# The maxima of two heads in four neighbouring rows of a score stack, returned by one transfer

## The chip, the core and the metric

The kernel runs on one core of a Trainium2 chip. The metric is the device time of one execution in microseconds (us). A core has five engines with their own instruction queues: TensorE (PE; its weight loads are listed apart as PEld), VectorE (DVE), ScalarE (ACT), GpSimd (POOL) and SyncE (SP). SP and ACT also issue the transfers between DRAM and the on-chip memory (SBUF), which 16 DMA engines carry out. Matmul results lie in PSUM.

## The reference, cut to what matters

```python
# A: attention over a sliding block of W = 256 keys, H = 32 heads of Dh = 16, S = 2048, D = 512
qkv = (x @ wqkv).reshape(B, S, 3, H, Dh)
scores = einsum("bhqd,bhkd->bhqk", q, k) * Dh ** -0.5
mask = (i - j >= 0) & (i - j < W)
p = softmax(where(mask, scores, -1e9))
a = einsum("bhqk,bhkd->bhqd", p, v) @ wo
# B: layer norm, Dense(1792), gelu, Dense(512)
b = gelu(layernorm(x) @ w1 + b1) @ w2 + b2
g = sigmoid((x * gate_w).sum(-1))
return g * a + (1 - g) * b
```

All inputs are float32. The softmax takes off each query's maximum; the change touches how these maxima reach the matmul that subtracts them.

## The kernel before

**Stages.** First come the projections (`qk_unit`, `v_unit`, L302 to L340), 12 matmuls of 128x512 each, and from 50 us on the first scores between them. From about 145 to 480 us run the attention of eight *head pairs* p (four heads each, two stacks of two heads) and, between its matmuls, the first layer of the MLP (`mlp1_unit`, L639). The rest is the second layer and the output projection. Numbers are held as a high and a low part of float32r, so each product is made of three matmuls.

**The stack.** `qk` (L166) is one SBUF tile of 128 partitions and four planes of 2048 columns: planes 0 and 1 hold q for the two stacks (`qs`), planes 2 and 3 hold k (`ks`). A head takes 48 partitions (three copies of 16 rows of high and low parts). In a plane the first head has partitions 14 to 61, the second 64 to 111. The two partitions behind a head's 48 belong to its maxima: in q the high and the low part of the maximum, in k the constant -1, so that the matmul of `st_pair` (L418: partitions 0 to 63 and 64 to 113) gives score minus maximum. `s_pair` (L362: 0 to 61 and 64 to 111) leaves those partitions out and gives plain scores, of which DVE takes the row maxima (L371, L372).

**Transfers.** The projections are written to the DRAM tiles `qkd[g, t]` (L162; t is 0 for q and 1 for k), eight heads of 50 rows each. `gaps` (L219) fills rows 48 and 49 of every head with -1, from partitions 112 to 127 of a k plane; it is issued once for each of four groups g. `load_stacks` (L344) brings the columns a to a + n of a head pair into the stack: 98 rows of DRAM (48, the two gap rows, 48) to partitions 14 to 111, both planes of t in one transfer, k first and then q. For the first pair there are four pairs of transfers of 512 columns, afterwards 56 pairs of 256 columns.

**The maxima.** Every four query blocks `put_max` (L376) runs a chain: `parts` splits 16 maxima of each of 128 partitions into high and low on POOL, `turn` transposes them on DVE, `put` writes them to a DRAM tile `md` (16 KB), and `rest` (L393 to L397) reads them back into the q planes, the high parts to partitions 62 and 112, the low ones to 63 and 113: two transfers of 8 KB, each with two outer rows. There are 32 such chains.

**Order.** In the attention stage the string `ORDER` sets the sequence of `s_pair` (S), `st_pair` (T), `pv` (P) and filler matmuls of the MLP (f). `CHAIN` gives the places after which the four steps of a chain are issued. `block` (L726) issues the stack loads of the next head pair at every second T block, and scores run ahead of T by `NB - LAG` = 10 blocks. All of SP's transfers go out in program order. A transfer reports on one of eight completion semaphores in turn (DMAHW0 to DMAHW7, shared by SP and ACT), and waits until the transfer eight places before it has landed.

Of the kernel before, what the change touches and what calls it, by code (L numbers as in the profile page):

```python
# [19 lines left out]
S = 2048  # L20
D = 512
H = 32
DH = 16
# [9 lines left out]
VW = 17  # L33
VR = 560
EPS = 1e-5
NEG = -3.0e38
# [25 lines left out]
def gated_mix_kernel(ctx, tc: tile.TileContext, xt, x2, wq0, wqk, wv, wo, xa, gw, w1, w2, b1, b2, out):  # L62
# [7 lines left out]
    def nm(s):  # L70
        uid[0] += 1
        return f"{s}_{uid[0]}"
# [56 lines left out]
    def f32(t):  # L129
        return t.bitcast(F32)  # L130
# [88 lines left out]
    def gaps(g):  # L219
        for t in range(2):  # L220
            sp.dma_start(f32(view(qkd[g, t], [50 * S, HG], [S, 2], [1, S], off=48 * S)), f32(ks[0][112:128]))

# [89 lines left out]
    def qk_out(g, t, c, o):  # L312
# [5 lines left out]
        def put(eng, k, s):  # L318
            eng.dma_start(f32(view(d, [S, DH], [50 * S, HG], [1, C], off=k * DH * S + c * C)), f32(s))

# [6 lines left out]
    def double(g, c, t):  # L327
        fr, to = (f32(view(qkd[g, t], [S, DH], [50 * S, HG], [1, C], off=k * DH * S + c * C)) for k in (0, 1 + t))
        sp.dma_start(to, fr)
# [14 lines left out]
    def load_stacks(p, a, n):  # L344
        g, j = divmod(p, 2)
        held_cols[p] = a + n
        for t in (1, 0):
            src = view(qkd[g, t], [S, 98], [100 * S, 2], [1, n], off=4 * j * 50 * S + a)
            sp.dma_start(f32(qk[14:112, 2 * t:2 * t + 2, a:a + n]), f32(src))

    mxs, done = {}, set()

    def s_pair(p, qb, pr):
# [6 lines left out]
        for e in range(2):  # L360
            r, k = ((0, 62), (64, 112))[e]
            pe.matmul(o[:, e, :n], qs[pr][r:k, qb * 128:qb * 128 + 128], ks[pr][r:k, t0:t0 + n],  # L362
                      start=True, stop=True)
# [12 lines left out]
    def put_max(p, a):  # L376
        mx = mxs[p][:, :, :, a:a + 4]
        sm = {}
        md = dram.tile([2, 2, 2, 4, 128], F32R, name=nm("md"))

        def parts():
            m = sm["m"] = small("nm", 2, (128, 2, 2, 2, 4), F32R)
            pool.tensor_copy(m[:, 0], mx)
            lo_part(m[:, 1], mx, m[:, 0], pool)

# [7 lines left out]
        def rest():  # L393
            done.add(("m", p, a // 4))
            for k in range(2):
                src = view(md, [512, 2], [1024, 2], [1, 512], off=2048 * k)
                sp.dma_start(f32(qk[62 + k:113 + k:50, :2, a * 128:a * 128 + 512]), f32(src))  # L397

# [573 lines left out]
```

## Time and profile before

| | before |
|---|---|
| median of 3 runs | 688.86 us (688.81 to 690.28) |
| the profiled execution | 689.64 us; its span 687.8 us, granted clock 0.999 |
| DMA | 137.91 MB in 89620 packets, mean 200 GB/s |
| DVE L372, row maxima | 144.1 us busy, 208 of 693 ns |
| POOL L422, masks | 74.2, 62.2 and 49.3 us busy in its three groups |
| ACT L420, exponentials | 76.5, 66.2 and 50.7 us busy in its three groups |

The span is the time from the first to the last instruction on the core; the execution's own time also holds what lies around it. Busy time is the time in which an engine works on instructions. It does not tell which engine sets the end: that is read from the chain of work that ended last, and from what an engine waited for. In a group's row stand the line, engine and operation, what is written and read, the count, the busy time and the mean of one instruction, and the idle time ahead with what ended it. SPq and ACTq rows are instructions that issue transfers.

### The profile page before, as it was taken

How to read it: one execution, taken by the hardware profiler on the slowest of the kernel's cores; microseconds unless marked ns; L12 is line 12 of the kernel's file. 1: busy time of each engine (PE TensorE's matmuls, PEld its weight loads, DVE VectorE, ACT ScalarE, POOL GpSimd, SP SyncE). 2: the span in 40 equal slices, each digit the busy share in tenths (PEclk: the TensorE clock that was granted, in tenths of full speed). 3: DMA queues.
4: the chain of work that ended last, by engine and by line, in shares of the span. 5: the costliest groups of instructions: out<-in, count | busy, mean ns of one | idle time of the engine just before them, and what ended most of it. 6: DMA issues, size and time to landing. Idle time of an engine off the chain costs nothing.

```text
span 687.8 us, 15593 instructions
## 1 busy us (share of the span) xinstructions
PE 681.1 (99%) x5674; PEld 535.5 (78%) x5674; DVE 476.4 (69%) x970; ACT 384.6 (56%) x637; POOL 265.9 (39%) x622
## 2 busy tenths in 40 slices
PE   9999999999999999999999999999999999999997
PEld 6887777877768777877787777777787888888886
DVE  6737789968777787777686877855575545556454
ACT  6438453457677776877758777687633224123231
POOL 6800156426666664765656566568000000000000
PEclk9999999999999999999999999999999999999999
DMA  8998888786575767566676555527876450841801
GB/s 322 354 290 266 278 262 267 217 253 224 176 211 173 247 211 228 174 214 188 190 240 207 168 185 153 178 96 240 288 238 204 143 173 5 275 126 41 253 1 62
DMA packets 89620, 137.91 MB, mean 200 GB/s; under 512 B 13160, under 2 KB 36648, under 8 KB 89416
## 3 DMA queue, kind: packets, MB, share of 16 engines
q1 hardware_dynamic: 81384, 128.72, 59.1%
q10 hardware_dynamic: 8160, 8.19, 3.9%
q8 instruction: 45, 0.74, 0.4%
q14 instruction: 31, 0.25, 0.1%
HBM read 81.53 MB, written 54.30 MB: 197 GB/s over the span
## 4 chain that ended last, share of the span: by engine, by line
PE 96%; ACT 1%; DVE 1%; DMA 1%; issue 0%; POOL 0%; SPq 0%; DVEq 0%; ACTq 0%
PE ps_b L651 22%; PE ps_a L881 22%; PE ps_b L441 13%; PE ps_d L308 12%; PE ps_b L418 7%; PE ps_b L362 7%; PE ps_d L338 7%; PE ps_o L850 6%; PE ps_d L295 1%; PE ps_x L362 1%; DMA qk<-qk 1%; PE ps_x L279 1%; ACT x L420 0%; DVE us L895 0%; DVE us L889 0%; ACT pb L420 0%
## 5 line engine op out<-in xcount | busy, mean ns | idle before, releaser
L651 PE MATMUL ps_b<-x,w 64*128 64x512 f32 x1344 | 207.1, 393 | 0.0
L881 PE MATMUL ps_a<-x,t 128*128 128x512 f32 x648 | 150.2, 389 | 0.2 <-DVE t L711 0.2
L372 DVE TENSOR_REDUCE mx<-ps_b 128x2 f32<-128x512 f32 x208 | 144.1, 693 | 7.1
L881 PEld LDWEIGHTS ps_a<-x,t 128*128 128x128 f32 x648 | 121.5, 188 | 26.2 <-DVE t L711 0.6
L651 PEld LDWEIGHTS ps_b<-x,w 64*128 64x128 f32 x1344 | 127.4, 186 | 10.5 <-ACT x L136 0.3
L371 DVE COPY_PREDICATED ps_b<-tri,ps_b 128x256 f32<-128x256 uint8 x208 | 88.4, 425 | 52.7 <-PE ps_b L362 40.6
L422 POOL TENSOR_SCALAR_AFFINE_SELECT pa<-pa 128x256 f32<-128x256 f32 x192 | 74.2, 414 | 57.7 <-ACT pa L420 56.7
L420 ACT ACTIVATE pa<-ps_b 128x768 f32<-128x768 f32 x96 | 76.5, 813 | 24.7 <-PE ps_b L418 13.3
L418 PE MATMUL ps_b<-qk 50*128 50x384 f32 (+5 forms) x512 | 87.8, 339 | 0.1
L308 PE MATMUL ps_d<-x,w 128*128 128x512 f32 x360 | 84.7, 390 | 0.0
L362 PE MATMUL ps_b<-qk 62*128 62x384 f32 (+3 forms) x472 | 83.0, 345 | 1.0 <-DMA qk<-qk 0.8
L308 PEld LDWEIGHTS ps_d<-x,w 128*128 128x128 f32 x360 | 67.3, 188 | 14.5 <-issue 0.5
L420 ACT ACTIVATE pb<-ps_b 128x768 f32<-128x768 f32 (+2 forms) x96 | 66.2, 706 | 20.5 <-PE ps_b L418 9.7
L422 POOL TENSOR_SCALAR_AFFINE_SELECT pb<-pb 128x256 f32<-128x256 f32 x160 | 62.2, 415 | 37.4 <-ACT pb L420 36.9
L707 ACT ACTIVATE t<-t,b1s 128x512 f32<-128x512 f32 x56 | 38.6, 716 | 44.0 <-DMA t<-hp 43.6
L418 PEld LDWEIGHTS ps_b<-qk 50*128 50x128 f32 (+1 forms) x512 | 48.8, 184 | 16.0 <-issue 3.2
L422 POOL TENSOR_SCALAR_AFFINE_SELECT x<-x 128x256 f32<-128x256 f32 x128 | 49.3, 414 | 29.7 <-ACT x L420 29.3
L420 ACT ACTIVATE x<-ps_b 128x768 f32<-128x768 f32 x64 | 50.7, 813 | 14.0 <-PE ps_b L418 9.7
L362 PEld LDWEIGHTS ps_b<-qk 62*128 62x128 f32 (+1 forms) x472 | 45.1, 184 | 17.2 <-issue 3.9
L338 PE MATMUL ps_d<-wv,x 128*128 128x512 f32 x192 | 46.7, 394 | 0.0
L850 PE MATMUL ps_o<-w,t 128*128 128x512 f32 x192 | 46.1, 389 | 0.0
L441 PE MATMUL ps_b<-pa,v 128*32 128x128 f32 (+2 forms) x704 | 42.9, 345 | 0.3 <-ACT x L420 0.2
(96 smaller groups left out, 757.1 us busy)
## 6 DMA issues: line engine op xcount, KB each, us to landing
qk<-qk SPq DMA_DIRECT2D x112, 196.0 KB
t<-hp SPq DMA_DIRECT2D x56, 256.0 KB
hp<-t SPq DMA_DIRECT2D x54, 256.0 KB
qk<-t SPq DMA_DIRECT2D x48, 256.0 KB
osc<-x SPq DMA_DIRECT2D x31, 256.0 KB
t<-in_w SPq DMA_DIRECT2D x28, 256.0 KB
w<-w SPq DMA_DIRECT2D x28, 256.0 KB
qk<-t ACTq DMA_DIRECT2D x24, 256.0 KB
```

The source lines that it names most:

```text
L308: pe.matmul(o, a[:, dt * 128:(dt + 1) * 128], b[:, dt * C:(dt + 1) * C], start=n == 0, stop=n == 11)
L338: pe.matmul(o, x[:, a:a + 128], wvs[dt][:, k], start=n == 0, stop=n == 11)
L362: pe.matmul(o[:, e, :n], qs[pr][r:k, qb * 128:qb * 128 + 128], ks[pr][r:k, t0:t0 + n], start=True, stop=True)
L371: dve.copy_predicated(o[:, :, :128], tri, o[:, :, 256:384])
L372: dve.tensor_reduce(m, o[:, :, :256], mybir.AxisListType.X, ALU.max)
L418: pe.matmul(o[:, e, :w], ks[pr][r:k, kb * 128:kb * 128 + 128], qs[pr][r:k, kb * 128:kb * 128 + w], start=True, stop=True)
L420: act.activation(pt[:, :, :w], o[:, :, :w], AF.Exp, scale=0.25)
L422: pool.affine_select(out=pt[:, :, a:a + 128], in_=pt[:, :, a:a + 128], pattern=[[0, 2], [sgn, 128]], base=b, channel_multiplier=-sgn, comp ...
L441: pe.matmul(a[32 * h:32 * h + 32, at:at + w], vs[:, kb, v:v + 32], pts[p, kb][:, h, fr:fr + w], start=n == 0, stop=n == len(parts) - 1, sk ...
L651: pe.matmul(o[:, e], w[kt // 4][r:r + 64, k, m:m + 128], y[r:r + 64, a:a + C], start=n == 0, stop=n == 23)
L850: pe.matmul(a, x[:, g], wos[g][:, k], start=n == 0, stop=n == 11)
L881: pe.matmul(accs[c][b], x[:, b * 128:(b + 1) * 128], w, start=f == 0 and n == 0, stop=f == FT - 1 and n == 2)
```

## The change

A head gets 52 rows in DRAM in place of 50 (`HR`), and of two neighbouring heads only the first one's four spare rows are used. A stack load brings 100 rows to partitions 14 to 113: 48, four spare ones, 48. The second head's data thereby lie in partitions 66 to 113, and partitions 62 to 65 hold high and low part of the first head's maximum and high and low part of the second's. `s_pair` takes partitions 64 to 113 for the second head, so its spare rows have to be 0 in q (t = 0): `gaps` now fills q's with zeros and k's with -1, by transfers of 4 x 2 rows of 4096 elements where there were 8 x 2 of 2048. `parts` writes its results in the order head, part, stack, block, so `md` is four rows of 4 KB and `rest` is one transfer of 16 KB.

```diff
+HR = 52
@@
-    qkd = {(g, t): dram.tile([HG, 50, S], F32R, name=f"qk{g}_{t}") for g in range(NG) for t in range(2)}
+    qkd = {(g, t): dram.tile([HG, HR, S], F32R, name=f"qk{g}_{t}") for g in range(NG) for t in range(2)}
@@ def gaps(g):
-            sp.dma_start(f32(view(qkd[g, t], [50 * S, HG], [S, 2], [1, S], off=48 * S)), f32(ks[0][112:128]))
+            dst = view(qkd[g, t], [2 * HR * S, 4], [2 * S, 2], [1, 2 * S], off=48 * S)
+            sp.dma_start(f32(dst), f32(qk[116 * t:116 * t + 8, 2:].rearrange("k r s -> k (r s)")))
@@ def load_stacks(p, a, n):
-            src = view(qkd[g, t], [S, 98], [100 * S, 2], [1, n], off=4 * j * 50 * S + a)
-            sp.dma_start(f32(qk[14:112, 2 * t:2 * t + 2, a:a + n]), f32(src))
+            src = view(qkd[g, t], [S, 100], [2 * HR * S, 2], [1, n], off=4 * j * HR * S + a)
+            sp.dma_start(f32(qk[14:114, 2 * t:2 * t + 2, a:a + n]), f32(src))
@@ def s_pair(p, qb, pr):
-            r, k = ((0, 62), (64, 112))[e]
+            r, k = ((0, 62), (64, 114))[e]
@@ def put_max(p, a):
-        md = dram.tile([2, 2, 2, 4, 128], F32R, name=nm("md"))
+        md = dram.tile([4, 2, 4, 128], F32R, name=nm("md"))
...
-            pool.tensor_copy(m[:, 0], mx)
-            lo_part(m[:, 1], mx, m[:, 0], pool)
+            mt = mx.rearrange("p r e b -> p e r b")
+            pool.tensor_copy(m[:, :, 0], mt)
+            lo_part(m[:, :, 1], mt, m[:, :, 0], pool)
...
-            for k in range(2):
-                src = view(md, [512, 2], [1024, 2], [1, 512], off=2048 * k)
-                sp.dma_start(f32(qk[62 + k:113 + k:50, :2, a * 128:a * 128 + 512]), f32(src))
+            sp.dma_start(f32(qk[62:66, :2, a * 128:a * 128 + 512]), f32(view(md, [1024, 4], [512, 2], [1, 512])))
```

In `qk_out` and `double` only the head's pitch changes, 50 to `HR`. Three places show what the instructions become. Rows give the line, what is written and read, and the outer sizes of the transfer; line numbers move by one to three between the two programs.

The first is SP's queue in the projection stage, at the first gap fill (L221; `qk_79` is the stack, `qk_0_65` and `qk_1_66` are the DRAM tiles of q and k of group 0). Before:

```order
L319 DMA qk_1_66<-t_347 16x8x512 [waits DMAHW1_49]
L319 DMA qk_1_66<-t_348 16x8x512 [waits DMAHW2_49,DVE_49]
L221 DMA qk_0_65<-qk_79 8x2x2048 [waits DMAHW3_49,Pool_49]
L221 DMA qk_1_66<-qk_79 8x2x2048 [waits DMAHW4_49]
L228 DMA t_399<-in_wqk 128x512 [waits DMAHW5_49]
```

Now:

```order
L321 DMA qk_1_66<-t_347 16x8x512 [waits DMAHW1_49]
L321 DMA qk_1_66<-t_348 16x8x512 [waits DMAHW2_49,DVE_49]
L223 DMA qk_0_65<-qk_79 4x2x4096 [waits DMAHW3_49,Pool_49]
L223 DMA qk_1_66<-qk_79 4x2x4096 [waits DMAHW4_49,Pool_49]
L230 DMA t_399<-in_wqk 128x512 [waits DMAHW5_49]
```

Nothing has moved; the two fills have four outer rows instead of eight.

The second place follows soon after on SP: the first stack loads (L349), which the first score matmuls on PE wait for. Before:

```order
L468 DMA t_448<-in_xa 128x512 [waits DMAHW0_49]
L349 DMA qk_79<-qk_1_66 98x2x512 [waits DMAHW1_49,Pool_49]
L349 DMA qk_79<-qk_0_65 98x2x512 [waits DMAHW2_49]
L468 DMA t_468<-in_xa 128x512 [waits DMAHW3_49,PE_49]
L228 DMA t_471<-in_wqk 128x512 [waits DMAHW4_49]
```

Now:

```order
L469 DMA t_448<-in_xa 128x512 [waits DMAHW0_49]
L351 DMA qk_79<-qk_1_66 100x2x512 [waits DMAHW1_49]
L351 DMA qk_79<-qk_0_65 100x2x512 [waits DMAHW2_49]
L469 DMA t_468<-in_xa 128x512 [waits DMAHW3_49,PE_49]
L230 DMA t_471<-in_wqk 128x512 [waits DMAHW4_49]
```

The order is the same, and the loads have 100 outer rows. On ACT's queue the next user of the second load's semaphore, DMAHW2, is a transfer of the projections (L319); these are ACT's rows before:

```order
L471 ACTIVATE waste_100,mv<-t_423 128x512 [waits DMAHW3_49]
L472 ACTIVATE waste_100,mv<-t_423,mv 128x512 [waits Activation_49]
L136 ACTIVATE t_530<-ps_d_517 128x512 [waits DMAHW0_49,DVE_49,PE_49]
L319 DMA qk_1_68<-t_530 16x8x512 [waits DMAHW2_49,Activation_49]
L471 ACTIVATE waste_100,mv<-t_448 128x512 [waits DMAHW0_49]
```

The third place is SP in the attention stage, where a chain's return (L397) stands between stack loads and other transfers (L541: a weight of the MLP; L664: a result of its first layer). Before:

```order
L349 DMA qk_79<-qk_1_68 98x2x256 [waits DMAHW4_49,PE_49]
L349 DMA qk_79<-qk_0_67 98x2x256 [waits DMAHW5_49]
L329 DMA qk_1_70<-qk_1_70 16x8x512 [waits DMAHW6_49]
L397 DMA qk_79<-md_2937 2x2x512 [waits DMAHW7_49,DMAHW3_49]
L397 DMA qk_79<-md_2937 2x2x512 [waits DMAHW0_49]
L541 DMA t_3057<-in_w 128x512 [waits DMAHW1_49]
L664 DMA hp<-t_3059 128x512 [waits DMAHW2_49,Activation_49]
```

Now:

```order
L351 DMA qk_79<-qk_1_68 100x2x256 [waits DMAHW2_49,PE_49]
L351 DMA qk_79<-qk_0_67 100x2x256 [waits DMAHW3_49]
L331 DMA qk_1_70<-qk_1_70 16x8x512 [waits DMAHW4_49]
L398 DMA qk_79<-md_2927 4x2x512 [waits DMAHW5_49,DMAHW1_49]
L542 DMA t_3046<-in_w 128x512 [waits DMAHW6_49]
L665 DMA hp<-t_3048 128x512 [waits DMAHW7_49,Activation_49]
```

The two returns have become one, and the transfers behind it stand one place earlier in the turn of the semaphores. SP has 572 rows where it had 604. On the other engines the order is unchanged; the two POOL instructions of `parts` work on 128x2x8 in place of 128x16 elements, and at four of the 32 returns a semaphore of PE is added, for the score matmuls that now read partitions 64 and 65.

More of the change, by code (lines that the diff above doesn't have):

```diff
@@ L327, in double @@
     def double(g, c, t):
[L328 removed]
+        fr, to = (f32(view(qkd[g, t], [S, DH], [HR * S, HG], [1, C], off=k * DH * S + c * C)) for k in (0, 1 + t))
         sp.dma_start(to, fr)
```

2 lines of the change are left out of this document (1 added, 1 removed).

## The prediction

> **What bounds the kernel now.** The first view is the page: busy time by engine, the chain that ended last, and the row of the score matmuls.
>
> ```profile
> PE 681.1 (99%) x5674; PEld 535.5 (78%) x5674; DVE 476.4 (69%) x970; ACT 384.6 (56%) x637; POOL 265.9 (39%) x622
> PE 96%; ACT 1%; DVE 1%; DMA 1%; issue 0%; POOL 0%; SPq 0%; DVEq 0%; ACTq 0%
> L362 PE MATMUL ps_b<-qk 62*128 62x384 f32 (+3 forms) x472 | 83.0, 345 | 1.0 <-DMA qk<-qk 0.8
> ```
>
> TensorE (PE) is busy 681.1 us of a span of 687.8, so 6.7 us are all that removing waits could win, and whatever makes PE wait is paid in full. The second view, PE's waits, says for what it stands still:
>
> ```profile
> PE ps_x L279 <- DVE t L275: 1.3, 1, 1.3
> PE ps_b L362 <- DMA qk<-qk: 0.8, 1, 0.8
> PE ps_b L441 <- ACT x L420: 0.2, 1, 0.2
> PE ps_a L881 <- DVE t L711: 0.2, 1, 0.2
> ```
>
> That is 2.5 us, and one wait of 0.8 is for something the change touches: the load of a stack (q and k rows of a head pair, DRAM to SBUF) ahead of a score matmul, L362. No row has PE waiting for the maxima (md). So the question is less what is saved than whether the transfers that feed PE arrive later.
>
> **The part that it is named for.** The third view groups what touches the stack; the wait row is SyncE's (SP) own.
>
> ```profile
> L349 SPq DMA_DIRECT2D qk<-qk x120: 308/411/2010, 40.7 to 447.5; - x120
> L397 SPq DMA_DIRECT2D qk<-md x64: 596/636/972, 81.3 to 465.8; - x64
> SPq L397 <- DMA md<-ms: 36.1, 21, 4.0
> ```
>
> 64 returns become 32, so SP issues 32 x 0.636 = 20.4 us less in some 385 us. SP is not on the chain and PE waits for none of these returns: I price this at 0. Each maximum may lie in place about 0.64 us sooner, since its second issue is gone; nobody stands waiting for it. The added semaphore on PE at the return (four of 32) asks for score matmuls that the maxima themselves were made from, so it is past when the return is issued. What could queue behind it on SP are the next stack loads.
>
> On GpSimd the two steps that make the maxima read 2 x 8 in place of 16 numbers; before, they take 0.20 and 0.22 us:
>
> ```profile
> 223.69 0.20 POOL L383 CAST nm<-mx 128x16 fp32r<-128x16 f32 x1
> 223.97 0.22 POOL L133 TENSOR_TENSOR nm<-mx,nm 128x16 fp32r<-128x16 f32 x1
> ```
>
> Were they to double, that is 32 x 0.42 = 13 us on an engine that is busy 39%: 0. The second head's score matmul takes 50 rows in place of 48. By form, 48 and 62 rows take the same:
>
> ```profile
> L362 PE MATMUL ps_b<-qk 62*128 62x384 f32 x208 | 72.4, 354 | 1.0 <-DMA qk<-qk 0.8
> L362 PE MATMUL ps_b<-qk 48*128 48x384 f32 x208 | 72.4, 354 | 0.0
> ```
>
> So 50 rows cost 0.
>
> **The part that it brings along: two other transfers change shape.** The stack load goes from 98 rows to 100, and the gap fill (L221) from 8 outer rows, 16 rows on its SBUF side, to 4 and 8 rows twice as long. The bytes hardly change (+2% and none). But what does the rate go by? I looked for stretches in which one kind of transfer is nearly alone: transfers of 128 rows (14 to 28 us), the last gap fills, and two stack loads. The rows of issue stand ahead; the last two columns of the windows are the mean busy share of the 16 DMA engines and GB/s.
>
> ```profile
> 78.14 1.37 SPq L221 DMA_DIRECT2D qk<-qk  x2
> 188.93 0.98 SPq L349 DMA_DIRECT2D qk<-qk  x2
> 14.00:28.00 14.00, 14.00 (x63) 11.60 (x62) 13.01 (x18) 6.13 (x12) 12.64 (x15) 1.00 1.05 395
> 82.50:84.00 1.50, 1.50 (x8) 1.21 (x7) 1.47 (x5) 0.00 (x0) 0.00 (x0) 1.00 0.50 182
> 191.40:191.90 0.50, 0.50 (x14) 0.32 (x16) 0.46 (x2) 0.50 (x1) 0.00 (x0) 1.00 0.89 313
> ```
>
> All engines and 395 GB/s with 128 rows; half of them and 182 GB/s with 8; 0.89 of them and 313 GB/s with 98. Eight of 16 is 0.50, and 14 of 16 is 0.875: 8 and 14 are the largest numbers up to 16 that divide 8 and 98. Read so, 100 rows go over 10 engines and 4 rows over 4. This is an inference from three points. The bounds of the unknown rates: a 100-row load runs between the wide rate (395, a gain) and that of the 8-row fill (182); the 4-row fill between 182 and half of it, 91. I take 313 x 10/14 = 224 and 91 GB/s, since these follow the pattern of the rows.
>
> The Trainium skill (DMA: Bandwidth & Descriptors, section "Why a DMA increments its semaphore by 16 and not by 1") states it as a rule: a transfer uses the largest number of engines up to 16 that divides the slowest dimension of both sides, and it names 100 partitions as giving 10. It speaks against this change, and the shares 0.50 and 0.89 agree with it. By the rule the terms below stand as they are; without it the load would cost its 2% of bytes and the sum would be about 0.
>
> **Term 1, the first stack pair.** Early in the program DMA is the crowded resource. SP, ACT and PE rows around it, then windows:
>
> ```profile
> 28.77 1.50 SPq L221 DMA_DIRECT2D qk<-qk  x2
> 40.74 0.88 SPq L349 DMA_DIRECT2D qk<-qk  x2
> L319 ACTq EVENT_SEMAPHORE  x1: 17/17/17, 49.4 to 49.4; - x1
> 49.93 0.33 PE L362 MATMUL ps_x<-qk 62*128 62x128 f32 x2
> 32.00:34.00 2.00, 2.00 (x11) 1.65 (x10) 0.33 (x1) 0.28 (x1) 1.15 (x1) 1.00 0.78 184
> 36.00:40.00 4.00, 4.00 (x19) 3.32 (x18) 1.12 (x2) 1.21 (x2) 0.00 (x0) 1.00 0.84 197
> 40.00:44.00 4.00, 4.00 (x20) 3.30 (x19) 1.72 (x3) 0.60 (x1) 0.00 (x0) 1.00 0.97 345
> 44.00:48.00 4.00, 4.00 (x19) 3.33 (x18) 1.12 (x2) 2.02 (x5) 0.00 (x0) 1.00 0.99 250
> ```
>
> ACT's transfer at 49.4 reuses the completion semaphore of the second stack load (DMAHW2 in the order shown above), so that load has landed at 49.4, 8.2 us after its issue, and the first score matmul starts at 49.93. The lead is 0.5 us. Ahead of it:
> - The gap fills: 2 x 131,072 bytes at 182 GB/s take 1.44 us, at 91 take 2.88: +1.44 on the engines that carry them, and the later wide transfers need those too. The windows show 2 x 0.22 + 4 x 0.16 = 1.08 us of idle DMA in between; I let a third of it, 0.4, catch up: +1.04. Bounds: 0 to 1.44.
> - The pair itself: 2 x 401,408 bytes at 313 GB/s take 2.56 us; 2 x 409,600 at 224 take 3.66: +1.10. Bounds: at 395 it is -0.5, at 182 +1.9.
>
> Together 2.14 later, less the lead of 0.5: PE waits **1.6 us** that it does not wait now. Bounds: 0 to 2.8. This delay then moves everything behind it, and it gives the next loads as much lead as it takes.
>
> **Term 2, the pair that is late already.** Four views of one place, SP's row, its wait, the chain, and PE:
>
> ```profile
> 222.32 2.14 SPq L349 DMA_DIRECT2D qk<-qk  x4
> SPq L664 <- ACT pb L420: 0.4, 1, 0.4
> 222.80 5.36 DMA qk<-qk
> 228.29 0.44 PE L362 MATMUL ps_b<-qk 62*128 62x384 f32 x2 [0.79 <-DMA qk<-qk]
> ```
>
> A pair of 2 x 200,704 bytes at 313 GB/s takes 1.28 us; 2 x 204,800 at 224 take 1.83: +0.55. SP is not sooner here, although a return is gone from 219.4: the transfer just ahead (L664) waits for ACT. So PE's wait grows from 0.79 by **0.55 us** (bounds -0.3 at 395 GB/s, +0.97 at 182).
>
> **Term 3, the other 54 pairs after the first head pair's start.** Each lands 0.55 us later, and PE waits for none of them now. Bounds: 0, if each has that lead, to 54 x 0.55 = 30 us, if none has. About half (28) follow one of the 32 returns on SP and get back up to 0.64. I take **0.3 us**, near the wait table, where 55 of 56 pairs come in time.
>
> Sum: 1.6 + 0.55 + 0.3 = 2.45 us, so a span of 690.3 where it was 687.8. The profiled execution took 689.64 with its launch, 0.78 above the median of 688.86; by the median it is 688.86 + 2.45 = **691.3 us**. A measurement of this kernel can tell about 0.2% (1.4 us) from no change.
>
> **The rivals.**
> 1. *The narrow transfers are hidden* (27%). The idle DMA time of 32 to 40 us takes up the whole 1.44, the load runs near the 313 GB/s that it has now, and PE waits as before. For it: SP's 20 us of relief, 55 of 56 pairs in time, and the share of 0.89 that comes from a short window. Against it: the lead of 0.5 and shares of 0.97 and 0.99. Time: 688.9 to 689.6; not slower by what can be told.
> 2. *Ten engines become a general limit* (12%). Loads come in bursts of four (222.32), each burst needs 1.1 us more of the same ten engines, and the leads are used up. If a third of the 54 pairs cost 0.3 us each it is 5.4 more: 696.7. It decides where the lead is under 0.5 us. Against it: a DMA share of 0.67 and 0.60 in the two halves of attention.
> 3. *Coalescing pays* (6%): the shorter return empties SP early enough that the stack loads leave sooner, and the 0.8 wait goes: 688.86 - 0.8 = 688.1, the most that PE's waits allow. It needs loads that queue right behind a return, and a load as fast as now. The Trainium skill (same page, "Rules for kernel authors") advises joining small transfers, since under 64 KB overhead is nearly all; by that rule alone the change gains here, and the absent md row in PE's waits shows that the gain falls where nobody waits.
>
> ```profile
> 145.00:300.00 155.00, 153.72 (x1892) 117.82 (x1892) 121.35 (x281) 114.01 (x175) 94.91 (x253) 1.00 0.67 209
> 300.00:480.00 180.00, 179.81 (x2216) 138.46 (x2212) 133.99 (x294) 131.83 (x203) 112.92 (x296) 1.00 0.60 187
> ```
>
> **How the numbers follow.** The forecast has 55% and spans 690.0 (the fills' delay caught up in full, term 3 nil: 0.6 + 0.55) to 693.0 (the upper bounds of terms 1 and 2, with term 3). Slower by over 0.2% (above 690.24): the forecast without its low end, 0.50, and rival 2, 0.12: 0.62. Within 0.2%: rivals 1 and 3 nearly whole and the low end, 0.35. Faster: 0.03, since it would take more than the waits hold. The range: 688.5 (rival 1, and a part of 3) to 693.5 (the forecast's top and the low end of rival 2).
>
> **What would show it.** Right: PE's waits get a row L362 on the qk loads with two entries or more, one at about 50 us of 1 to 2.5 us; the window of two stack loads shows a share near 0.63 and 220 to 230 GB/s in place of 0.89 and 313; that of the last gap fills 0.25 and 91; the return's row counts 32. Term 1 falls if the first score matmul still starts at 49.9 without a wait; term 2 if the wait at 228 stays at 0.8; term 3 if other waits for qk sum to over 1 us. The whole is wrong if the share in the load's window stays at 0.89.

## The result and the profile after

| | before | after |
|---|---|---|
| median | 689.07 us (687.98 to 690.28, 6 runs) | 698.31 us (696.76 to 701.18, 6 runs) |
| ratio | | 1.0138, interval 1.0113 to 1.0162 |
| profiled execution, its span | 689.64 us, 687.8 us | 699.84 us, 698.1 us |
| granted clock, mean | 0.999 | 0.993 |

The change makes the kernel 9.2 us slower where 2.45 us were forecast; the range given ended at 693.5 us. Waits, clock and busy times below are those of one profiled execution each. The page of after: busy times, and TensorE's granted clock in each fortieth of the span (9 is 90% or more of the full clock):

```profile
PE 685.7 (98%) x5674; PEld 537.6 (77%) x5674; DVE 473.5 (68%) x970; ACT 384.2 (55%) x637; POOL 267.0 (38%) x622
PEclk9999998999999999999999999999999999999999
```

TensorE is busy 685.7 us where it was 681.1, with the same 5674 matmuls: 4.6 us of the loss are the same work done more slowly. The one lower digit of the clock, the seventh, says where most of it is, at 105 to 122 us. The idle rest is 12.4 us (698.1 - 685.7) in place of 6.7: 5.7 us are waits. Both together are the 10.3 us by which the spans differ. TensorE's waits in after (total, count, longest):

```profile
PE ps_x L364 <- DVE mx L374: 3.2, 2, 2.8
PE ps_x L364 <- DMA t<-in_xa: 2.6, 1, 2.6
PE ps_x L281 <- DVE t L277: 1.3, 1, 1.3
PE ps_a L882 <- DVE t L712: 0.5, 2, 0.4
PE ps_b L442 <- POOL pb L423: 0.4, 1, 0.4
PE ps_b L442 <- ACT x L421: 0.2, 1, 0.2
```

Two rows are new, and both end at score matmuls (L364). The row of 0.8 us for a stack load in the attention stage is gone. The timeline shows where the two stand:

```profile
52.53 0.44 PE L364 MATMUL ps_x<-qk 62*128 62x128 f32 x4 [2.61 <-DMA t<-in_xa]
105.68 0.69 PE L364 MATMUL ps_x<-qk 62*128 62x384 f32 x2 [2.78 <-DVE mx L374]
106.74 0.69 PE L364 MATMUL ps_x<-qk 62*128 62x384 f32 x2 [0.38 <-DVE mx L374]
```

The first is the place of term 1, the first score matmul. Its bracket names another load that landed last by the profile; the chain of waits names the stack load, with its time from issue to landing:

```profile
42.30 10.09 DMA qk<-qk
```

The second, near 103 us, is for row maxima on DVE (L374) and was in no step of the prediction. What follows the waits is seen in windows of 3.41 us: first TensorE's busy time, and in the last three columns the clock, the DMA share and GB/s.

```profile
50.59:54.00 3.41, 1.47 (x9) 1.25 (x10) 0.00 (x0) 0.91 (x3) 0.00 (x0) 0.99 0.86 300
54.00:57.41 3.41, 3.41 (x10) 2.64 (x9) 3.08 (x7) 3.02 (x8) 0.00 (x0) 0.51 0.89 281
101.79:105.20 3.41, 1.11 (x5) 0.57 (x4) 3.31 (x9) 2.42 (x6) 1.51 (x4) 0.99 0.77 219
105.20:108.61 3.41, 2.56 (x7) 1.70 (x8) 3.38 (x7) 0.80 (x3) 2.67 (x10) 0.50 0.72 171
108.61:112.02 3.41, 3.41 (x9) 2.64 (x9) 3.15 (x7) 0.34 (x1) 1.82 (x3) 0.51 0.89 255
```

After each wait the clock stands at one half for whole windows. Half of the busy time at half clock is lost: (3.41 + 2.56 + 3.41) / 2 = 4.7 us, the 4.6 of the page. So there are two episodes: near 50 us 2.6 of wait and 1.7 of clock, near 103 us 2.8 + 0.4 of wait and 3.0 of clock, 10.5 us together; the other waits about cancel.

The parts that the prediction named for the transfers are the last gap fills in the microsecond with the least beside them, the end of a stack load that is nearly alone, and SP's row of the returns:

```profile
91.00:92.00 1.00, 1.00 (x7) 0.81 (x6) 0.96 (x3) 0.00 (x0) 0.00 (x0) 1.00 0.33 92
395.20:395.60 0.40, 0.40 (x6) 0.36 (x6) 0.40 (x1) 0.24 (x1) 0.40 (x2) 1.00 0.66 233
L398 SPq DMA_DIRECT2D qk<-md x32: 610/677/1161, 89.2 to 474.5; - x32
```

A share of 0.33 and 92 GB/s for the fills where the forecast was 0.25 and 91, 0.66 and 233 for a load (0.63 and 220 to 230), and 32 returns. The loads' windows also hold other transfers; the completion events in the trace are plainer. A load has 11 of them, one early and ten at its end, where before it has one and 14; a fill has one and four, before one and eight. Read as one event for each engine, that is the 10 and 14, 4 and 8 engines of the prediction.

### The profile page after: what moved, and what is told of

It reads as the page before. It is cut to its first block, busy times and chain, and to the rows that moved or that the text cites. A ratio compares the mean times of both kernels' runs of the same rounds, so it can differ in the third digit from the quotient of the medians.

```text
span 698.1 us, 15568 instructions
## 1 busy us (share of the span) xinstructions
PE 685.7 (98%) x5674; PEld 537.6 (77%) x5674; DVE 473.5 (68%) x970; ACT 384.2 (55%) x637; POOL 267.0 (38%) x622
## 4 chain that ended last, share of the span: by engine, by line
PE 85%; DMA 9%; DVE 3%; ACT 1%; issue 1%; SPq 0%; ACTq 0%; POOL 0%; DVEq 0%
PE ps_b L652 22%; PE ps_a L882 19%; PE ps_b L442 12%; PE ps_b L419 7%; PE ps_b L364 6%; PE ps_d L310 6%; PE ps_o L851 6%; PE ps_d L340 4%; DMA t<-in_x 2%; DMA qk<-t 1%; DMA qk<-qk 1%; DMA t<-hp 1%; DMA t<-in_xa 1%; DMA gws<-in_gw 1%; PE ps_d L297 1%
## 5 line engine op out<-in xcount | busy, mean ns | idle before, releaser
L374 DVE TENSOR_REDUCE mx<-ps_b 128x2 f32<-128x512 f32 x208 | 144.0, 692 | 7.2
L419 PE MATMUL ps_b<-qk 64*128 64x384 f32 (+5 forms) x512 | 88.0, 339 | 0.1
L310 PE MATMUL ps_d<-x,w 128*128 128x512 f32 x360 | 86.4, 396 | 0.0
L364 PE MATMUL ps_b<-qk 62*128 62x384 f32 (+3 forms) x472 | 82.8, 344 | 0.1
L421 ACT ACTIVATE pb<-ps_b 128x768 f32<-128x768 f32 (+2 forms) x96 | 66.2, 706 | 20.1 <-PE ps_b L419 12.4
L364 PEld LDWEIGHTS ps_b<-qk 62*128 62x128 f32 (+1 forms) x472 | 44.8, 184 | 15.9 <-issue 3.9
L340 PE MATMUL ps_d<-wv,x 128*128 128x512 f32 x192 | 48.9, 407 | 0.0
L340 PEld LDWEIGHTS ps_d<-wv,x 128*128 128x128 f32 x192 | 37.3, 197 | 9.5 <-issue 1.5
```

What stands on the lines that cost most here:

```text
L310: pe.matmul(o, a[:, dt * 128:(dt + 1) * 128], b[:, dt * C:(dt + 1) * C], start=n == 0, stop=n == 11)
L340: pe.matmul(o, x[:, a:a + 128], wvs[dt][:, k], start=n == 0, stop=n == 11)
L374: dve.tensor_reduce(m, o[:, :, :256], mybir.AxisListType.X, ALU.max)
L419: pe.matmul(o[:, e, :w], ks[pr][r:k, kb * 128:kb * 128 + 128], qs[pr][r:k, kb * 128:kb * 128 + w], start=True, stop=True)
L421: act.activation(pt[:, :, :w], o[:, :, :w], AF.Exp, scale=0.25)
```

## The experiments

The question was which of the two reshaped transfers makes which episode, whether the return has a price, and why a wait costs clock. Ratios are to the kernel before, measured beside each kernel. Diffs are cut: of those with + lines alone, the lines replace the two of `gaps` or of the load that the change put there.

**Each part put into the kernel before.** First the fills alone, on four engines, in pieces of 4 KB where before has 8 KB:

```diff
-sp.dma_start(f32(view(qkd[g, t], [50 * S, HG], [S, 2], [1, S], off=48 * S)), f32(ks[0][112:128]))
+sp.dma_start(f32(view(qkd[g, t], [S // 2, 4], [50 * S, HG], [1, S // 2], off=48 * S)), f32(ks[0][112:128]))
```

> The kernel before, with the gap fills dealt out by four column blocks in place of eight heads; loads of 98 rows and two returns as before. Theory F: 696 to 699 us, with waits of PE near 52 and 106 us. Theory L: 689 us, no new wait over 0.5 us. Theory S: one wait of about 0.9 us near 50 us (1.4 less the lead of 0.5), 690 to 692 us.

Measured: 690.16 us, ratio 1.0010 (0.9996 to 1.0023). No change that can be told. Then the loads alone, 100 rows:

```diff
-            src = view(qkd[g, t], [S, 98], [100 * S, 2], [1, n], off=4 * j * 50 * S + a)
-            sp.dma_start(f32(qk[14:112, 2 * t:2 * t + 2, a:a + n]), f32(src))
+            src = view(qkd[g, t], [S, 100], [100 * S, 2], [1, n], off=4 * j * 50 * S + a)
+            sp.dma_start(f32(qk[14:114, 2 * t:2 * t + 2, a:a + n]), f32(src))
```

> The kernel before, with stack loads of 100 rows in place of 98: the second head's two gap rows come along, its maxima overwrite them as before. Fills of eight heads and two returns as before. Theory F: 689 to 690 us. Theory L: 696 to 699 us. Theory S: a wait of about 0.6 to 1 us near 50 us (1.1 less 0.5), and the wait at 228 us larger than 0.8: 690 to 692 us. DMA share in a window of two loads near 0.63 by the reading of ten engines, 0.89 if rows do not matter.

Measured: 695.87 us, 1.0082 (1.0049 to 1.0116). TensorE's first score matmul in this kernel's timeline:

```profile
52.39 0.44 PE L362 MATMUL ps_x<-qk 62*128 62x128 f32 x4 [2.71 <-DMA qk<-qk]
```

The loads alone make the first episode (2.61 us in after). They do more here: at 169 us, in the attention stage, TensorE waits 2.4 us for a stack load, and the next window is at half clock.

```profile
PE ps_b L362 <- DMA qk<-qk: 2.4, 1, 2.4
169.09:172.50 3.41, 3.41 (x36) 1.76 (x36) 1.12 (x2) 0.81 (x1) 0.77 (x2) 0.50 0.87 310
```

Both edits together:

> The kernel before with both: fills by four column blocks, loads of 100 rows; two returns as before. All three theories: the loss of the change comes back without the single return, 696 to 699 us. If instead the layout of 52 rows, the return or the order of the semaphores matter, it stays below 694 us.

Measured: 695.91 us, 1.0085 (1.0067 to 1.0102): no more than the loads alone. So these short-pieced fills add nothing to the time, and something of the changed kernel was still missing from this one. With 99 rows, one row more than before, a load has one completion event and 11 at its end, so 11 engines:

```diff
-            src = view(qkd[g, t], [S, 98], [100 * S, 2], [1, n], off=4 * j * 50 * S + a)
-            sp.dma_start(f32(qk[14:112, 2 * t:2 * t + 2, a:a + n]), f32(src))
+            src = view(qkd[g, t], [S, 99], [100 * S, 2], [1, n], off=4 * j * 50 * S + a)
+            sp.dma_start(f32(qk[14:113, 2 * t:2 * t + 2, a:a + n]), f32(src))
```

> The kernel before with stack loads of 99 rows in place of 98 (one of the second head's gap rows comes along); all else as before. By the divisor reading 11 engines in place of 14: the first load lands 1.5 to 3 us later, PE waits 1 to 2.5 us near 50 us, 692 to 696 us. If the loss of 100 rows goes by bytes or by partitions past 111, 99 rows cost next to nothing: 689 to 690.5 us.

Measured: 692.05 us, 1.0047 (1.0027 to 1.0067). The loss is 3.2 us. All loads together move 25.7 MB, and 1% of that at the mean 200 GB/s would be 1.3 us (an estimate) even if none of it were hidden, so it is not the bytes alone. The profiled execution (span 688.1 us) shows one new wait, of 0.5 us; where the others lost their time it can't show.

**The changed kernel with other fills.** Eight engines and pieces of 4 KB, in place of four and 16 KB:

```diff
-            dst = view(qkd[g, t], [2 * HR * S, 4], [2 * S, 2], [1, 2 * S], off=48 * S)
+            dst = view(qkd[g, t], [S // 2, 8], [2 * HR * S, 4], [1, S // 2], off=48 * S)
```

> The changed kernel, with the gap fills dealt out by eight column blocks in place of four heads; the same values go to the same rows. Theory F (the fills on four engines are the cause): the waits of 2.6 us at 52 us and of 2.8 us at 106 us go, and with them both stretches at half the PE clock, so about 689 us. Theory L (the stack loads of 100 rows are the cause): the waits stay within half a us, 697 to 699 us. Theory S (the two add up against a lead of 0.5 us): the first wait shrinks by about 1.4 us to 1.2, the second goes or shrinks by half, 691 to 694 us.

Measured: 694.80 us, 1.0060 (1.0042 to 1.0078). In the profiled execution the two waits fall to 1.0 and 1.4 us, and the clock does not drop. Then 16 engines and pieces of 256 bytes, from constant tiles of 128 partitions:

```diff
-    get("edge", "edge", 1, (128, 120))
+    edge = get("edge", "edge", 1, (128, 120))
...
+        pool.memset(edge, -1.0)
...
+            src = (wide.bitcast(F32) if not t else edge)[:, :64].unsqueeze(1).to_broadcast([128, 4, 64])
+            sp.dma_start(f32(view(qkd[g, t], [64, 128], [2 * HR * S, 4], [1, 64], off=48 * S)), src)
```

> The changed kernel, with the gap fills taken from 128 partitions in runs of 64 elements, so that they have 128 rows on both sides; loads stay at 100 rows. Theory L (the loads of 100 rows are too slow by themselves): 693 to 696 us, as with fills in eight blocks (694.8). If what is left there still comes from the fills: 689 to 691 us.

Measured: 689.98 us, 1.0013 (0.9996 to 1.0030). With the 100-row loads and the single return still there, nothing of the loss can be told any more. In the kernel before the same fills:

> The kernel before with one edit: its gap fills, 8 rows of 16 KB, go out from all 128 partitions of a constant tile in pieces of 256 bytes; everything else, the 98-row loads and the two returns, stays. Theory E (narrow transfers add up on the low-numbered DMA engines): before, the loads go over 14 engines and the fills over 8, and no wait of over 0.8 us hung on either, so there is nothing left to gain: 688 to 689.5 us, a ratio of 0.999 to 1.001. Rival (the fills hold the projection stage up in before as well): faster by 0.3% or more, under 687. Rival (small pieces are dear): slower, over 690.5, with the first stack pair's wait near 50 us grown.

Measured: 689.19 us, 0.9997 (0.9981 to 1.0012): before has nothing to gain from them. Next, four engines kept and only the pieces cut to 4 KB:

```diff
+            for k in range(2):
+                dst = view(qkd[g, t], [S // 2, 4], [2 * HR * S, 4], [1, S // 2], off=(48 + 2 * k) * S)
+                sp.dma_start(f32(dst), f32(qk[116 * t:116 * t + 8, 2 + k]))
```

> The changed kernel with its fills cut into pieces of 4 KB that still go over four engines, from the same 8 source rows (four column blocks of 1024 for each stack row, the columns in two transfers, so 16 fills in place of 8). Against the changed kernel only the length of a piece changes (16 KB to 4 KB), against after_fill8 only the engines (8 to 4). Theory E (bytes per engine count): as the changed kernel, 696.5 to 700 us, ratio 1.010 to 1.016. Rival L (a long piece blocks its engine for others): as after_fill8 and before_both, 693.5 to 696 us, ratio 1.006 to 1.010.

Measured: 694.77 us, 1.0064 (1.0041 to 1.0086), the time of after_fill8 with its eight engines. So the count of engines alone does not set what the fills cost. The two kernels lose their time in different ways, though: here the first wait is 0.5 us, and the second episode still stands, with both of its half-clock windows.

```profile
PE ps_x L365 <- DVE mx L375: 2.6, 2, 2.0
PE ps_x L365 <- DMA qk<-qk: 0.5, 1, 0.5
102.59:106.00 3.41, 2.96 (x8) 2.18 (x9) 3.18 (x7) 1.12 (x2) 3.00 (x8) 0.50 0.88 246
106.00:109.42 3.42, 3.42 (x10) 2.65 (x9) 3.35 (x7) 0.24 (x1) 1.32 (x2) 0.50 0.94 313
```

The mean granted clock was 0.994 to 0.997 in all six of its runs, in those of after_fill8 0.995 to 1.000. With pieces of 8 KB:

```diff
+            dst = view(qkd[g, t], [S, 4], [2 * HR * S, 4], [1, S], off=48 * S)
```

> The changed kernel with the fills in pieces of 8 KB over four engines as in after_fill4k, but read from the 8 source rows of the changed kernel in place of 4 rows read four times each. It tells why after_fill4k was at 715 us, where its 8 KB pieces took 1106 ns each against 909 ns for 16 KB in the changed kernel. Theory (few source rows are slow to read): back to 697 to 700 us, pieces of 8 KB near 450 ns. Rival (column blocks as the outer dimension write to DRAM badly): still over 710, pieces near 1100 ns.

Measured: 698.23 us, 1.0118 (1.0091 to 1.0144), between, with waits of 1.3 and 2.7 us in the trace. Another kernel with pieces of 8 KB reads its constants from four rows, four times each:

```diff
+            src = qk[116 * t:116 * t + 4, 2].unsqueeze(1).to_broadcast([4, 4, S])
+            sp.dma_start(f32(view(qkd[g, t], [S, 4], [2 * HR * S, 4], [1, S], off=48 * S)), f32(src))
```

> The changed kernel with the fills still on four engines, but cut along the columns: four column blocks of 8 KB for each of the four stack rows sets, so pieces of 8 KB where the changed kernel has 16 KB, and the same bytes. It tells the count of engines from the length of a piece. Theory E (it is the four engines that queue): as the changed kernel, 697 to 699.5 us, ratio over 1.011, with the waits near 50 and 105 us of over 2 us each. Rival (it is the 16 KB pieces that block an engine for other transfers): near after_fill8 and before_both, 694 to 696 us, and no stretch at half clock.

Measured: 715.13 us, 1.0377 (1.0355 to 1.0399), which neither theory expected. With eight source rows (after_fill4k8) it is gone, so it was the source, not the length.

Is it the length of a piece, then, that the fills cost by? The trace has a rival: the time for which the fills hold each of their engines, that is, the times of all their pieces, added up and divided by the engines. It puts these kernels, which all load 100 rows, in the same order, and after_fill4k too, which the length does not:

| fills | pieces, engines | time on each engine | ratio |
|---|---|---|---|
| after_fill16 | 256 bytes, 16 | 4.6 us | 1.0013 |
| after_fill8 | 4 KB, 8 | 12.2 us | 1.0060 |
| after_fill4x4 | 4 KB, 4 | 14.5 us | 1.0064 |
| after_fill4k8 | 8 KB, 4 | 16.5 us | 1.0118 |
| after | 16 KB, 4 | 17.8 us | 1.0138 |
| after_fill4k | 8 KB, 4 | 32.3 us | 1.0377 |

The fills of before hold their eight engines for 9.8 us. No run changes the length alone at an equal time, so which of the two it is stays open.

**The changed kernel with other loads.** On top of after_fill8, each load as two of 52 and 48 rows (13 and 16 engines):

```diff
+            for r, k in ((0, 52), (52, 48)):
+                src = view(qkd[g, t], [S, k], [2 * HR * S, 2], [1, n], off=(4 * j * HR + r) * S + a)
+                sp.dma_start(f32(qk[14 + r:14 + r + k, 2 * t:2 * t + 2, a:a + n]), f32(src))
```

> The changed kernel with fills in eight column blocks, and each stack load in two transfers of 52 and 48 rows in place of one of 100 (by the divisor reading 13 and 16 engines in place of 10), the same bytes to the same places; 120 issues more on SP, some 50 us of its time. Theory L: the waits for qk near 50 us and the late DVE near 102 us go, 689 to 691 us. If not the width but the bytes, the rows' places or the order matter: 694 to 697 us, and SP's issues may add to it.

Measured: 693.20 us, 1.0067 (1.0043 to 1.0092), no gain over 1.0060. Doubling the number of transfers and widening them was one edit here, so it says little on the width. On top of after_fill16:

> The changed kernel with the fills from 128 partitions and each load of 100 rows as two, of 52 and 48 rows (13 and 16 engines). Theory E: with both narrow transfers wide again nothing of the change's cost is left: 688 to 690 us, ratio 0.999 to 1.002, and no wait of over 1 us at the first stack pair. Rival (each load's issue costs more than its engines give, as after_split's 693.2 against after_fill8's 694.8 leaves open): over 690.5, with queue waits of SP.

Measured: 690.22 us, 1.0015 (0.9990 to 1.0040). The width by itself was tried by loading 98 of the 100 rows:

```diff
-            src = view(qkd[g, t], [S, 100], [2 * HR * S, 2], [1, n], off=4 * j * HR * S + a)
-            sp.dma_start(f32(qk[14:114, 2 * t:2 * t + 2, a:a + n]), f32(src))
+            src = view(qkd[g, t], [S, 98], [2 * HR * S, 2], [1, n], off=(4 * j * HR + 2) * S + a)
+            sp.dma_start(f32(qk[16:114, 2 * t:2 * t + 2, a:a + n]), f32(src))
```

> The changed kernel whose loads bring 98 of the 100 stack rows, so that a load goes over 14 engines again in place of 10; the first two rows of each stack half are not loaded and stay at the constant they were set to, so this part of the first head's scores is left out. Row order, fills (16 KB pieces, four engines) and the single return stay as changed. Theory (the loads' ten engines and the fills' long pieces are both needed for the loss): 690 to 693 us, ratio 1.001 to 1.005, and no wait of over 1.5 us at the first stack pair. Rival (the fills' long pieces are the loss by themselves, as after_split's 1.0067 beside after_fill8's 1.0060 suggests, where wider loads gained nothing): 696 us or more, ratio 1.009 or over.

Measured: 694.49 us, 1.0077 (1.0062 to 1.0093), between the two expectations. TensorE's timeline and two windows of this kernel:

```profile
49.71 0.44 PE L364 MATMUL ps_x<-qk 62*128 62x128 f32 x4
102.16 0.69 PE L364 MATMUL ps_x<-qk 62*128 62x384 f32 x2 [3.62 <-DVE mx L374]
97.47:100.88 3.41, 1.07 (x5) 0.56 (x3) 3.34 (x9) 1.62 (x5) 0.63 (x1) 1.00 0.72 204
100.88:104.29 3.41, 1.76 (x5) 1.09 (x6) 3.34 (x8) 0.82 (x2) 2.61 (x9) 0.51 0.81 191
```

This takes the two apart: with 14 engines for a load the first episode is gone, the second is there in full. The two are worth 1.0138 - 1.0077 = 0.61% (the loads) and 0.77% (the rest) in this kernel; put into before, the loads cost 0.82%. The 98 rows go to partitions 16 to 113 here, so it is not the partitions past 111 either.

**The return.** On the changed kernel it was made two transfers again:

```diff
-            sp.dma_start(f32(qk[62:66, :2, a * 128:a * 128 + 512]), f32(view(md, [1024, 4], [512, 2], [1, 512])))
+            for k in range(2):
+                src = view(md, [1024, 2], [512, 2], [1, 512], off=2048 * k)
+                sp.dma_start(f32(qk[62 + 2 * k:64 + 2 * k, :2, a * 128:a * 128 + 512]), f32(src))
```

> The changed kernel with the return of a block as two transfers of two rows, 8 KB each, as before; the stack's row order, the loads of 100 rows and the fills stay as changed. It prices the one transfer in place of two by itself. Theory: the returns are hidden, so as the changed kernel, 697 to 700 us. Rival (fewer returns do pay, as fill16_ret2's 691.6 against after_fill16's 690.0 could mean): 1.5 us or more slower, over 700.5. Rival (the single return over four engines is part of the loss): 696 or under.

Measured: 700.59 us, 1.0140 (1.0119 to 1.0161), against 1.0138 with one transfer. Up to the first return, at 89 us in after, this kernel makes the same transfers as after, and yet its first wait is 1.1 us in place of 2.6, with no half clock behind it:

```profile
PE ps_x L364 <- DVE mx L374: 4.6, 4, 3.4
PE ps_x L364 <- DMA qk<-qk: 1.1, 1, 1.1
```

So the first episode differs from execution to execution; the second, with its 3.4 us and two half-clock windows, is there again. The same on after_fill16:

> The changed kernel with the fills from 128 partitions (as in after_fill16) and the return of a block as two transfers of two rows each, 8 KB a transfer as before, in place of the one of four rows. It differs from after_fill16 in the count of returns alone, so it prices what the change was about. Theory: the returns are hidden, the one transfer saves nothing and costs nothing: the time of after_fill16, 690 us within 1. Rival (fewer returns pay and lay under the other costs): slower than after_fill16 by 0.3% or more, 692 or over. Rival (the single return over four engines is what after_fill16 still pays against before): faster, 689 or under.

Measured: 691.64 us, 1.0034 (1.0016 to 1.0052), against 1.0013 (0.9996 to 1.0030). The second pair leans to a gain of 0.2% by the single return, with overlapping intervals; the first shows none. TensorE does wait for returned maxima in some of these kernels, 2.0 us in before_both and 1.9 in fill16_split, though in neither before nor after.

**A later demand.** Scores of the first head pair one unit later, so that their loads have more lead:

```diff
-        at((16, 18, 20, 22, 24, 26, 29, 32, 35, 38)[qb], lambda qb=qb: [s_pair(0, qb, pr) for pr in range(2)])
+        at((17, 19, 21, 23, 25, 27, 30, 33, 36, 39)[qb], lambda qb=qb: [s_pair(0, qb, pr) for pr in range(2)])
```

> The changed kernel with each of the ten first score pairs one projection unit (2.7 us) later; transfers untouched. Theory P (the loss is paid where a score matmul stands in line ahead of a load that is 0.5 us from late, and the clock's half-speed stretches follow from these waits): the waits near 52 and 106 us and both half-speed stretches go, 689 to 692 us. If the transfers cost elsewhere, or the half-speed stretches have another cause: 694 us or more, with the stretches still there.

Measured: 703.59 us, 1.0208 (1.0175 to 1.0241): slower still. The first score matmul, now at 52.65 us, waits for nothing, but waits of 2.9, 2.2 and 2.1 us stand near 60, 100 and 178 us, the first two for row maxima on DVE, the third for a stack load. Waiting longer for one load does not help the rest; that the maxima come later and make DVE late is the likely reason, and was not tested.

**Waits of a known length.** In the second layer of the kernel before, at the three borders between column chunks, ACT copies a finished accumulator into the next one, two times or four times, before TensorE may go on:

```diff
             accs[c] = [ps(f"a{(4 * c + b) % 6}") for b in range(4)]
+            for _ in range(2 if c else 0):
+                act.copy(accs[c][0], accs[c - 1][3])
```

> The kernel before with an extra wait of TensorE at three places of the second layer's last loop, where its four column chunks meet: ACT copies the finished accumulator of one chunk into the first accumulator of the next, twice in a row, before TensorE may start there. A copy of 128x512 took 0.59 us from PSUM in the profile, so a wait of some 1.4 us at each place, 4.2 us in all. The copied values are overwritten. Theory G (only waits of about 2.1 us and more are followed by a half-speed clock, as in the profiles so far): no stretch at clock 0.5 at these places, 4 to 5 us slower than before, a ratio of 1.006 to 1.0075. Rival (any wait costs clock): 1.009 or more.

> As gate_short, with four copies in a row: a wait of some 2.6 to 2.8 us at each of the three places, some 8 us in all. Theory G: each wait is followed by a stretch of 3.41 us or 6.83 us at clock 0.5 that costs 1.7 to 3.4 us more, so 13 to 18 us slower than before, a ratio of 1.019 to 1.026, more than twice gate_short's loss. Rival (a wait costs its length, and the half clock in the earlier profiles had another cause): 8 to 8.5 us, a ratio of 1.0115 to 1.0125.

Measured: 700.59 us, 1.0166 (1.0142 to 1.0190), and 708.09 us, 1.0263 (1.0246 to 1.0280). The waits came out longer than planned: 6.4, 2.05 and 2.05 us with two copies, 7.4, 3.25 and 3.25 with four, since at the first border ACT itself stood 6.8 us for DVE. First the kernel with two copies, timeline and windows:

```profile
595.69 3.86 PE L883 MATMUL ps_a<-x,t 128*128 128x512 f32 x10 [2.05 <-ACT ps_a L878]
648.63 3.69 PE L883 MATMUL ps_a<-x,t 128*128 128x512 f32 x15 [2.05 <-ACT ps_a L878]
593.19:596.60 3.41, 1.36 (x6) 0.81 (x6) 3.34 (x7) 2.10 (x4) 0.00 (x0) 1.00 1.00 357
596.60:600.01 3.41, 3.41 (x10) 2.66 (x9) 3.04 (x6) 0.90 (x2) 0.00 (x0) 0.50 0.87 272
644.39:647.80 3.41, 2.19 (x10) 1.50 (x8) 3.19 (x6) 0.40 (x1) 0.00 (x0) 1.00 0.62 177
647.80:651.21 3.41, 2.58 (x11) 2.17 (x12) 3.31 (x7) 2.61 (x5) 0.00 (x0) 1.00 0.85 318
651.21:654.62 3.41, 3.41 (x16) 2.83 (x16) 1.44 (x3) 0.00 (x0) 0.00 (x0) 1.00 0.94 246
```

Two waits of the same length, 2.05 us: the first lies in one window of 3.41 us and the next window runs at half clock, the second is cut by a border at 647.80 and nothing follows. The same in the kernel with four copies:

```profile
651.88 1.43 PE L883 MATMUL ps_a<-x,t 128*128 128x512 f32 x5 [3.25 <-ACT ps_a L878]
646.80:650.20 3.40, 1.82 (x9) 1.17 (x7) 3.37 (x6) 0.72 (x2) 0.00 (x0) 1.00 0.72 228
650.20:653.61 3.41, 1.73 (x8) 1.43 (x9) 2.39 (x6) 3.35 (x6) 0.00 (x0) 1.00 0.94 314
653.61:657.03 3.42, 3.42 (x17) 2.84 (x16) 2.09 (x5) 0.44 (x2) 0.00 (x0) 1.00 0.89 243
```

A wait of 3.25 us, cut into 1.58 and 1.68 us, and the clock stays whole. So the theory that a wait's length decides falls, and the rival that any wait costs clock falls too: what decides is the idle share of a window whose borders stand fixed.

## Why the prediction was wrong

**The bound and the price of the return: right.** The return's 20 us of SP time were worth nothing that after_ret2 can tell (1.0140 against 1.0138). The matmul with 50 rows, POOL's two steps and the added semaphore show up in no wait of after.

**The inference of the engines: right.** 100 rows go over 10 engines, and 98, 99 and 100 rows in otherwise equal kernels gave 1, 1.0047 and 1.0082. The completion events (14, 11 and 10 at a load's end, eight and four at a fill's) bear out the rule of the Trainium skill that the prediction cited (DMA: Bandwidth & Descriptors, "Why a DMA increments its semaphore by 16 and not by 1"), and the times show that a single row can cost. **For the fills it named the right number and counted too little of what follows**: the rate was 92 GB/s as forecast, but of the eight fills it priced the first two, for what they delay ahead of the first stack load. What the later ones do was put at nothing.

**Term 1: 1.6 us of wait were forecast; 2.6 us and 1.7 us of clock came in after, 1.1 us and no loss of clock in after_ret2, whose transfers are the same up to there.** Its steps beside the trace's issue and landing times:

| second stack load of the first pair | issued | landed | from issue to landing | wait at the first score |
|---|---|---|---|---|
| before | 41.2 us | 49.4 us | 8.2 us | 0 |
| gate_short, the same program up to there | 40.0 | 47.5 | 7.5 | 0 |
| gate_long, likewise | 40.2 | 48.3 | 8.1 | 0 |
| after | 42.3 | 52.4 | 10.1 | 2.6 |
| after_ret2 | 42.0 | 50.8 | 8.8 | 1.1 |
| after_rows98 | 41.0 | 48.8 | 7.7 | 0 |
| after_fill16 | 39.8 | 49.6 | 9.8 | 0 |

The fills' step was +1.04. After's issue is 1.1 later than before's, but equal programs differ by up to 1.2 here; the means of the three kernels with each kind of fill differ by 1.3. The load's step was +1.10 and is larger: in the traces this load takes 7.5 to 8.2 us with 98 rows (six kernels) and 8.8 to 10.5 with 100 in one transfer (eleven), 1.7 more on the mean and close to the upper bound of 1.9 that the prediction had set and not taken. So the wait was sized about right, in part by luck given this scatter, and what it does to the clock was missing.

**The step that failed is what was left out behind term 1: "This delay then moves everything behind it, and it gives the next loads as much lead as it takes."** The second episode near 103 us is 6.2 of the 10.5 us. It hangs on the last fills, which the prediction put at nothing, and no delay gave it lead. The chain of waits of after leads back from it over DVE, and further to transfers for the layer norm (t<-in_x and t<-in_xa):

```profile
77.63 8.00 DMA t<-in_xa
86.88 8.41 DMA t<-in_x
95.31 3.95 DMA t<-in_x
99.28 0.69 DVE t L476 x2
104.84 0.69 DVE mx L374
```

The waits from 76 to 106 us of after say how it reaches DVE: ACT's sums (L472) stand 6.0 us for a row block of x, DVE (L476) stands 4.1 us for ACT, and the row maxima of the scores are queued behind it on DVE.

```profile
ACT waste L472 <- DMA t<-in_xa: 8.6, 3, 6.0
DVE t L476 <- ACT waste L473: 4.8, 2, 4.1
PE ps_x L364 <- DVE mx L374: 2.8, 1, 2.8
```

In after_fill16 the same rows from the same stretch (lines moved by one) are short, and TensorE has none:

```profile
ACT waste L473 <- DMA t<-in_xa: 2.9, 1, 2.9
DVE t L477 <- ACT waste L474: 1.7, 2, 1.0
```

The last fill landed at 93.2 us in after, at 84.4 in after_fill16, at 84.2 before. That the fills make this episode is shown: after_rows98 has it without the loads' change, and with after_fill16's fills it is gone. How they do it can be read from the completion events, of which a transfer of x has 16. In after, of the row block issued at 85.70 us, twelve come by 89.85 and the last four at 92.56, 92.91, 94.05 and 94.48. The four at the end of the last fill, issued just ahead at 84.35, come at 91.31, 91.63, 92.69 and 93.22, each 1.25 to 1.36 us ahead of one of those. In after_fill16 the last four are 0.7 us behind the twelfth (84.22 to 84.93); in before, whose fill uses eight engines, seven come by 83.41 and nine from 84.50 to 85.20. So in after four engines finish their part of x up to 4.6 us behind the others, and ACT's sum starts at 94.64, behind the last of them. The events do not name their engines; that these are the four of the fill is read from number and time. The prediction looked for PE's direct waits on qk alone, and not for what else uses the same engines at that time.

**The clock was left out.** TensorE's clock was in no term; it is 4.6 of the 10.3 us. Rival 2, which came closest in time (696.7), is not what happened in after: the loads of the attention stage make PE wait nowhere there. In before_rows100 one does, for 2.4 us, so it is not ruled out for other executions.

**Term 2 had the wrong sign, term 3 was about nothing.** The wait of 0.79 us at 228 us is gone, in after as in before_fill4. It also comes and goes without any change: in gate_short and gate_long, whose program is that of before up to 520 us, it is 1.6 us and nothing.

```profile
PE ps_b L362 <- DMA qk<-qk: 1.6, 1, 1.6
```

So one execution's wait was taken for the kernel's. (Its lower bound at 395 GB/s comes to -0.24, not -0.3.) Other waits for qk are not there in after.

**Not settled.** Whether the single return gains 0.2% once the loss is out (the after_fill16 pair leans that way), where before_rows99 lost its time, and whether fills cost by the length of a piece or by the time on their engines. A stack load of 104 or 112 rows, which by the same reading would go over 13 or 16 engines in one transfer, was not tried. No version beats the kernel before: after_fill16 (1.0013) and before_fill16 (0.9997) are equal to it within their intervals.

## What to carry over

A change of layout that spares transfers also changes the shape of those it leaves: look at the row counts (how many engines) and at the length of a contiguous piece of every transfer that it touches, so at how long it holds each of its engines, and at who else needs those engines at that time. In a stage where DMA is full, follow a late transfer to every engine that stands for it in order, not to TensorE's own waits alone. And price a new wait of TensorE of over about 1.7 us at its length plus 1.7 us for each window of 3.41 us that may then run at half clock, here 4.3 us for a wait of 2.6.

## What the runs showed of the hardware

- **The clock goes by idle share in fixed windows.** Cut into windows of 3.41 us on the borders that the clock's own changes show, the traces of all kernels here have 19 full-clock windows in which TensorE was idle for 56% or more: the next one was at half clock every time. After 13 windows with 30 to 45% it never was; of three windows at 46, 47 and 50%, two were followed. So 1.92 us of waiting cost clock in fill16_split, and 3.25 us in gate_long did not. The Trainium skill (TensorE: Matmul & The Clock Gate) says in its section "HAM oscillation — how this bites in real kernels" to avoid idle gaps of over about 3.4 us; that is too lenient here, since about half of a window was enough. In "What's actually happening" it says that the window of 3413 ns runs freely, and the borders here agree.
- **The same wait can therefore cost different amounts**, by where it falls: of two waits of 2.05 us in gate_short one was followed by half clock and one was not. How much of the spread between executions comes of this (before_rows100 had seven of its eight runs from 692.4 to 702.0 us, before all 19 from 688.3 to 692.8) was not measured.
- **Few source rows, read again and again, are slow.** Reading the constants from four partitions, four times each, a piece of 8 KB took 1106 ns (after_fill4k), from eight partitions once each 309 ns (after_fill4k8), both medians in the trace, on four engines and with the same destination. Added up the pieces took 129 us against 66. Whether the few rows or the repeated reading does it was not separated.
